# A Fourier mixing layer and a SoLU layer in one kernel: another order of work at its two ends

## The chip, the cores and the metric

The kernel runs on one core of one Trainium2 chip. The metric is the time of one execution on the device, in microseconds (us); the runs of a kernel are given by their median. The core has five engines with a queue of instructions each: TensorE (PE in the profile; its weight loads are PEld), VectorE (DVE), ScalarE (ACT), GpSimd (POOL) and SyncE (SP), which issues transfers. Every engine works through its own queue in the order in which the program puts instructions there, and waits where an instruction needs something that another engine or a transfer has not delivered.

## The reference: what is computed

```python
x:     (8, 3136, 256)                       # batch, sequence, features
X = np.fft.fft(np.fft.fft(x, axis=1), axis=2).real
x = X.reshape(8 * 3136, 256)                # 25088 tokens
h = x @ w_in                                # w_in (256, 1024)
e = np.exp(h - max(h))                      # along the 1024
solu = h * e / (sum(e) + 1e-09)
ln = (solu - mean(solu)) / sqrt(var(solu) + 1e-06) * g_ln
out = ln @ w_out                            # w_out (1024, 256)
```

The weights come as float64 from the host and are taken apart by bits on the chip; all arithmetic is in float32.

## The kernel before, in words

**Tiles and units.** The transform along the sequence is done in two steps (3136 = 49 x 64). The first (`transform1`, L184) multiplies by the table `F` and keeps its result in DRAM (`keep`, L221); `turn` (L224) brings it back with other rows on the partitions, as `g`. The second (`transform2`, L232) multiplies a piece of `g` by the table `T`. Batches are taken in four pairs, and each pair has 25 frequencies `k1`; a pair with a `k1` is a *unit*, so there are 100 units. A unit is 128 tokens and, by symmetry of the real transform, also the 128 tokens of the mirrored frequency: two *signs*, 0 and 1. Units with `k1` of 0 have only sign 0. The transform along the features is not computed: its matrix is multiplied into `w_in` beforehand (`product_in`, `keep_in`), with an even half (`Wi[:, 0]`), an odd half (`Wi[:, 1]`) and one row for the middle feature (`w_mid`).

**One unit.** `take2` (L246) copies the second transform from PSUM to `q`. `up(t, 0)` and `up(t, 1)` (L272) multiply `q` by the even and the odd half, into the PSUM tiles `h0` and `h1`, of which there is one each. `even` (L280) adds, on VectorE, the middle row times the column `t.r`; that column is a row of `q` turned on its side, either by a small transfer (`spread`, L250) or by a matmul (`column`, L265). `join` (L286) makes h of a sign from the even and odd parts and finds its maximum; `expo` (L294, ScalarE) takes exponentials; `product` (L302, VectorE) multiplies by h and sums; `square` (L309, ScalarE) sums squares and writes its result over h; `stats` (L316, ScalarE) and `power` (L332, GpSimd) give the factor 1/sqrt(var). The tiles `h` have two buffers, so the join of a sign waits for the square of the same sign one unit earlier (where both units have two signs).

**Down.** The product with `w_out` needs the unit's u turned. Units 0 to 3 (`WHOLE = 4`, L35) are turned by TensorE (`turn_whole`, L384), in four PSUM banks, which ScalarE and VectorE copy to `uT`. Later units are turned in blocks of 32 by VectorE (`turn_both`, L375), and transfers move the blocks (`move_blocks`, L401, by SP). The product itself runs five units behind (`lag = 5`, L825). For units with two signs it is done with seven block products instead of eight (class `Down`, L453: `p1` to `p7`), for which `sums` (L438, GpSimd) prepares four block sums of u and `weight_sums` (L421, GpSimd) four of `w_out`; `seed`, `keep_p`, `keep_x`, `keep_c` (ScalarE) and `finish` (VectorE) scale and combine. Units with one sign take a plain product (`down`, L513, and `scale`, L527). `store` (L531) writes sign 0 by SP and sign 1 by an indirect transfer of GpSimd.

**Centring.** The mean of `ln` is removed by taking the mean row from `w_out`: `centre` (L694) sums the 1024 rows with sixteen matmul records against a tile of ones, ScalarE scales the sum to `wbar` (L699), and VectorE subtracts it from all of `Wo` (L700).

**Weights.** `w_in` comes in four pieces and `w_out` in four; for each, `exponent` (L573) cuts out the exponent on VectorE, `confine` (L583) clips it, on ScalarE by three instructions or, with `here=True`, on VectorE by two, and `narrow` (L597) puts the float32 number together on VectorE.

**The order around the change** is written by hand (`manual_schedule`, L742); each engine's queue follows the program.
- L773-799: eight chunks of the first pair: load, add the mirrored rows, fold the features (VectorE), `transform1` (TensorE), a copy to `z` (ScalarE, L217).
- L801-824: `turn` of the first five `k1`, the rest of the weights, `transform2` and `take2` of units 0 and 1 with their `spread`, the rest of `keep`, the second table.
- L859-903: units 0 to 4. `begin(i + 1)` (L841) puts `up`, `column` for units 2 and 3, `even` and the next `transform2` into the queues in the middle of unit i. For the next pair `ahead` (L708) loads chunks, adds mirrored rows on GpSimd in halves, behind the last `product` of a unit given by `after` (`behind`, L719), and folds them on VectorE.
- L912-993: units 5 to 99 and five more rounds that only drain.

## Time and profile before

| what | us |
|---|---|
| median of 3 runs (lowest, highest) | 1136.63 (1136.53, 1139.17) |
| the profiled execution's own time | 1132.91 |
| its span in the profile | 1130.9 |
| TensorE busy in the span | 1092.3 |
| VectorE, ScalarE, GpSimd busy | 987.4, 800.5, 796.3 |
| TensorE in the first 47 us | 22.95 |
| TensorE's last matmul ends | 1125.8 |

The profile is of one execution. Its span starts and ends with the first and last instruction; the execution's own time is 2.0 us longer. The granted TensorE clock is 1.0. In a line of a timeline stand the start and the length in us, the engine, the line of the kernel, the operation, output and inputs, the shape, and in brackets how long the engine was idle before and what ended that. A float32 matmul leaves two records, so four records of 128x512 are the two matmuls of one `up`.

### The profile page before, as it was taken

How to read it: one execution, taken by the hardware profiler on the slowest of the kernel's cores; microseconds unless marked ns; L12 is line 12 of the kernel's file. 1: busy time of each engine (PE TensorE's matmuls, PEld its weight loads, DVE VectorE, ACT ScalarE, POOL GpSimd, SP SyncE). 2: the span in 40 equal slices, each digit the busy share in tenths (PEclk: the TensorE clock that was granted, in tenths of full speed). 3: DMA queues.
4: the chain of work that ended last, by engine and by line, in shares of the span. 5: the costliest groups of instructions: out<-in, count | busy, mean ns of one | idle time of the engine just before them, and what ended most of it. 6: DMA issues, size and time to landing. Idle time of an engine off the chain costs nothing.

```text
span 1130.9 us, 21944 instructions
## 1 busy us (share of the span) xinstructions
PE 1092.3 (97%) x7030; PEld 872.2 (77%) x7030; DVE 987.4 (87%) x1442; ACT 800.5 (71%) x1945; POOL 796.3 (70%) x698
## 2 busy tenths in 40 slices
PE   2898999999999999999999999999999999999998
PEld 1556787887887787878877787878877788778888
DVE  7889989898889998898988998898888899898983
ACT  4667777777767777777767777777776777777761
POOL 3036888875795988865878788876686576766673
PEclk9999999999999999999999999999999999999999
DMA  9672798766998879876969798876788685965665
GB/s 246 207 196 57 169 189 205 174 150 147 165 207 159 188 174 186 192 152 144 169 149 186 170 191 187 197 178 148 152 160 156 132 164 116 161 142 112 140 135 119
DMA packets 459601, 185.77 MB, mean 164 GB/s; under 512 B 426870, under 2 KB 441470, under 8 KB 459488
## 3 DMA queue, kind: packets, MB, share of 16 engines
q1 hardware_dynamic: 445728, 146.22, 63.0%
q0 software_dynamic: 13760, 38.16, 13.1%
q8 instruction: 57, 0.93, 0.3%
q14 instruction: 56, 0.46, 0.1%
HBM read 44.78 MB, written 38.80 MB: 74 GB/s over the span
## 4 chain that ended last, share of the span: by engine, by line
PE 90%; DVE 4%; issue 2%; ACT 2%; DMA 2%; SPq 0%; POOL 0%; POOLq 0%; DVEq 0%; ACTq 0%
PE ps_m L451 52%; PE ps_h L277 28%; PE ps_m L214 5%; PE ps_m L242 4%; DMA raw_in<-in_moe_w_in_dram 1%; DVE h L291 1%; DVE u L306 1%; PE ps_m L519 1%; ACT h L313 1%; DVE ev L283 0%; DVE y L150 0%; PE wps L665 0%; DVE Wo L615 0%; DVE y L149 0%; ACT u L299 0%
## 5 line engine op out<-in xcount | busy, mean ns | idle before, releaser
L277 PE MATMUL ps_h<-Wi,q 128*128 128x512 f32 x800 | 362.4, 594 | 5.9 <-DVE nmax L291 5.1
L444 POOL TENSOR_TENSOR S<-uT 128x512 f32<-128x512 f32 x186 | 238.0, 1279 | 108.3 <-DVE u L306 34.5
L451 PE MATMUL ps_m<-Ws,S 128*128 128x128 f32 x2304 | 296.4, 275 | 0.0
L451 PEld LDWEIGHTS ps_m<-Ws,S 128*128 128x128 f32 x2304 | 279.8, 192 | 3.6 <-issue 0.4
L313 ACT ACTIVATE h<-u,usum 128x1024 f32<-128x1024 f32 x196 | 225.3, 1150 | 79.5 <-DVE u L306 79.0
L277 PEld LDWEIGHTS ps_h<-Wi,q 128*128 128x128 f32 x800 | 143.8, 190 | 152.0 <-issue 139.4
L306 DVE SCALAR_TENSOR_TENSOR u<-h,u 128x1024 f32<-128x1024 f32 x196 | 234.7, 1234 | 9.4 <-ACT u L299 9.4
L299 ACT ACTIVATE u<-h,nmax 128x1024 f32<-128x1024 f32 x196 | 223.8, 1143 | 6.0 <-DVE nmax L291 4.7
L377 DVE STREAM_TRANSPOSE v<-u 128x2048 f32<-128x2048 f32 x88 | 203.4, 2311 | 3.1
L451 PE MATMUL ps_m<-Wo,uT 128*128 128x128 f32 x1536 | 203.7, 276 | 0.0
L451 PEld LDWEIGHTS ps_m<-Wo,uT 128*128 128x128 f32 x1536 | 187.9, 192 | 1.0 <-issue 1.0
L291 DVE CUSTOM_DVE_ANT_0 h<-ev,ps_h 128x1024 f32<-128x1024 f32 x100 | 122.2, 1222 | 17.0 <-DVE ev L283 8.8
L536 POOL DMA_INDIRECT out_dram<-ot,idx x96 | 109.7, 1143 | 37.4 <-issue 12.5
L291 DVE CUSTOM_DVE_ANT_0 h<-h,ps_h 128x1024 f32<-128x1024 f32 x96 | 117.2, 1221 | 14.2 <-DVE nmax L291 0.5
L283 DVE SCALAR_TENSOR_TENSOR ev<-w_mid,r,ps_h 128x1024 f32<-128x1024 f32 x100 | 124.1, 1241 | 0.8 <-PE ps_h L277 0.7
L444 POOL TENSOR_TENSOR S<-uT,S 128x512 f32<-128x512 f32 x93 | 118.8, 1278 | 7.3
L444 POOL TENSOR_TENSOR S<-S,uT 128x512 f32<-128x512 f32 x93 | 118.7, 1277 | 7.3
L451 PE MATMUL ps_m<-Wo,S 128*128 128x128 f32 x768 | 101.5, 275 | 0.8 <-ACT ot L486 0.8
L451 PE MATMUL ps_m<-Ws,uT 128*128 128x128 f32 x768 | 101.8, 276 | 0.0
L242 PEld LDWEIGHTS ps_m<-T,g 128*128 128x128 f32 x400 | 60.1, 191 | 50.1 <-issue 45.7
L451 PEld LDWEIGHTS ps_m<-Wo,S 128*128 128x128 f32 x768 | 93.4, 192 | 1.0 <-issue 1.0
L214 PE MATMUL ps_m<-y,F 98*100 98x258 f32 (+3 forms) x288 | 70.4, 377 | 24.4 <-DVE y L162 22.1
(103 smaller groups left out, 1177.7 us busy)
## 6 DMA issues: line engine op xcount, KB each, us to landing
uT<-v SPq DMA_DIRECT2D x752, 128.0 KB
g<-zd POOLq DMA_DIRECT2D x72, 160.0 KB, 5.2
out_dram<-ot SPq DMA_DIRECT2D x176, 64.0 KB
xa<-in_x_dram SPq DMA_DIRECT2D x28, 392.0 KB
zd<-z SPq DMA_DIRECT2D x24, 400.0 KB
raw_in<-in_moe_w_in_dram SPq DMA_DIRECT2D x4, 512.0 KB
raw_out<-in_moe_w_out_dram SPq DMA_DIRECT2D x2, 1024.0 KB
room<-in_x_dram SPq DMA_DIRECT2D x4, 392.0 KB
```

What stands on the lines that cost most here:

```text
L214: nc.tensor.matmul(o[..., cs], F[:, 2 * t + h, :], i[..., cs], start=first, stop=True, skip_group_check=True)
L242: nc.tensor.matmul(o, g[:, k, h * P : (h + 1) * P], table, start=(h == 0), stop=True, skip_group_check=True)
L277: nc.tensor.matmul(ps[:, fs], t.q[:, c * P : (c + 1) * P], Wi[:, c, fs], start=True, stop=True)
L283: nc.vector.scalar_tensor_tensor(out=t.ev, in0=w_mid, scalar=t.r, in1=ps, op0=ALU.mult, op1=ALU.add)
L291: nc.vector.tensor_tensor_reduce(out=t.h[s], in0=t.h[0] if s else t.ev, in1=t.odd, scale=1.0 if s else -0.5, scalar=3.0e38, op0=ALU.add, o ...
L299: nc.scalar.activation(out=t.u[s], in_=t.h[s], func=ACT.Exp, bias=t.nmax[:, s : s + 1], scale=-1.0, accum_out=t.esum[:, s : s + 1])
L306: t.last = nc.vector.scalar_tensor_tensor(out=t.u[s], in0=t.h[s], scalar=-1.0, in1=t.u[s], op0=ALU.mult, op1=ALU.mult, accum_out=t.usum[:, ...
L313: nc.scalar.activation(out=t.h[s], in_=t.u[s], func=ACT.Square, bias=t.usum[:, s : s + 1], scale=-float(FF), accum_out=t.ssq[:, s : s + 1])
L377: nc.vector.transpose(out=t.batch.v[:, :, t.w], in_=t.both.rearrange("p s (g n) -> p (s g) n", n=32))
L444: i = engine.tensor_tensor(out=S[j], in0=a, in1=b, op=op)
L451: nc.tensor.matmul(o, a[:, c], b[:, c], start=start and c == 0, stop=c == n - 1, skip_group_check=True)
L536: dma = nc.gpsimd.indirect_dma_start(out=out, out_offset=bass.IndirectOffsetOnAxis(ap=idx[:, i : i + 1], axis=0), in_=t.ot[s], in_offset=None)
```

## The change

It touches only the two ends of the program. In the queues:

- *Chunks.* In the last chunk VectorE takes two exponents of `w_out` instead of three, clips the first itself and narrows the first piece at once; the clipping of the second is done by ScalarE, one instruction ahead of each of the two copies of that chunk and one behind. `product_in(1)` is cut into four pieces: one after chunk 4, one after chunk 5, two after `turn`.
- *Before unit 0.* Both second transforms of units 0 and 1 (in two PSUM banks) come before the last clipping and the last three narrowings.
- *Mean row.* `fold_out` lets GpSimd add halves of `Wo` three times, 2048 columns to 256; `mean_out` is one matmul with ones on that, in round 1; `keep_mean` scales it on ScalarE behind the exponentials of unit 1; `centre` subtracts on GpSimd in four pieces, behind unit 1's last product. `weight_sums` moves to round 2, behind unit 2's last product.
- *ScalarE.* The turned unit 0 is copied behind unit 1's exponentials; `stats` of a unit moves one round later, behind the next unit's exponentials (units 0 and 1 both in round 2), and `power` to the end of that round.
- *Unit 5.* Its even part is finished by TensorE: two further matmuls with one row (`w_mid[0:1]`) add to the same PSUM tile, and ScalarE copies it to `ev`; this happens in round 4, and unit 5 has no `spread`.
- *Block sums of unit 1.* Two in round 3, two in round 4, instead of all in round 5. The additions of mirrored rows in rounds 3 and 4 stand behind the current unit's product.
- *Tail.* In round 100 the squares and `stats` of unit 99 come behind `keep_c`, its `power` in round 101; four of the sixteen moves of unit 98 are issued by GpSimd; for unit 99 `p7` and its half of `finish` come before `p3`.

The core of the diff:

```diff
+MIDDLE = (5,)
@@ column, up, even
-        ps = result(2)[:, 0:1]
+        ps = result(5 - t.k1)[:, 0:1]
...
+        whole_even = c == 0 and t.p == 0 and t.k1 in MIDDLE
...
+        if whole_even:
+            for half in range(2):
+                fs = slice(half * HW, (half + 1) * HW)
+                nc.tensor.matmul(ps[:, fs], t.q[0:1, P : 2 * P], w_mid[0:1, fs], start=False, stop=True)
...
+        if t.p == 0 and t.k1 in MIDDLE:
+            nc.scalar.copy(t.ev, ps)
+            return
@@ class Weights
-        def centre(self):
-
-            cs = result(0)[:, 0:D]
-            for c in range(KF):
-                nc.tensor.matmul(cs, ones, Wo[:, c, :], start=(c == 0), stop=(c == KF - 1))
-            nc.scalar.mul(out=wbar, in_=cs, mul=1.0 / FF)
-            nc.vector.tensor_tensor(out=Wo, in0=Wo, in1=wbar.unsqueeze(1).to_broadcast([P, KF, D]), op=ALU.subtract)
+        def fold_out(self):
+
+            half = Ws[:, 0:2].rearrange("p j c k -> p (j c k)")
+            quarter, eighth = [Ws[:, j].rearrange("p c k -> p (c k)") for j in (2, 3)]
+            w = Wo.rearrange("p c d -> p (c d)")
+            for o, i in ((half, w), (quarter, half), (eighth[:, 0:D], quarter)):
+                n = o.shape[1]
+                nc.gpsimd.tensor_tensor(out=o, in0=i[:, 0:n], in1=i[:, n : 2 * n], op=ALU.add)
+            self.part = eighth[:, 0:D]
+
+        def mean_out(self):
+            self.cs = result(3)[:, 0:D]
+            nc.tensor.matmul(self.cs, ones, self.part, start=True, stop=True)
+
+        def keep_mean(self):
+            nc.scalar.mul(out=wbar, in_=self.cs, mul=1.0 / FF)
+
+        def centre(self, t):
+
+            for c in range(0, KF, 2):
+                i = nc.gpsimd.tensor_tensor(out=Wo[:, c : c + 2], in0=Wo[:, c : c + 2],
+                                            in1=wbar.unsqueeze(1).to_broadcast([P, 2, D]), op=ALU.subtract)
+                if c == 0:
+                    behind(i, t)
@@ chunks and before unit 0
-                for i in range(3):
+                for i in range(2):
                     weights.exponent_out(i)
+                confine(weights.units[0], True)
+                weights.narrow_out(0)
...
+                if c == NC - 1:
+                    confine(weights.units[0], parts=(s,))
                 transform1(first, c * CH // 2 + s)
...
+        weights.product_in(1, (2, 3), odd)
         middle = weights.product_in(KD)
-        confine(weights.units[0], True)
-        for i in range(1, 3):
-            confine(weights.units[i])
+        confine(weights.units[0], parts=(2,))
+        for i in range(2, 4):
+            weights.exponent_out(i)
+        weights.keep_in(1, odd)
+        confine(weights.units[1])
         weights.keep_in(KD, middle)
...
+        for t, ps in [(t, transform2(pairs[0], t.k1, t.k1)) for t in units[:2]]:
+            take2(t, ps)
+            spread(t)
+        confine(weights.units[2])
         for i in range(1, 4):
             weights.narrow_out(i)
+        weights.fold_out()
@@ units 0 to 4
-                turn_whole(prv)
+                turn_whole(prv, i == 1)
+            if i == 1:
+                weights.mean_out()
...
+            if i == 1:
+                weights.keep_mean()
+            if i in (1, whole):
                 for o, ps in prv.wait:
                     nc.scalar.copy(o, ps)
...
+            done = units[0 if i == 2 else i - 1 : i] if i > 1 else []
+            for t in done:
+                stats(t)
+            if i == whole:
+                nxt = units[i + 1]
+                enter(i + 1)
+                even(nxt, up(nxt, 0))
...
             if i == 1:
-                weights.centre()
-                weight_sums()
+                weights.centre(cur)
+            if i == 2:
+                weight_sums(cur)
...
+            if i == whole - 1:
+                sums(units[1], None, part=slice(0, 2))
+            for t in done:
+                power(t)
@@ units 5 to 99 and the tail
-            if i == len(units):
-                for s in prv.signs:
-                    square(prv, s)
-            if prv:
+            if prv and cur:
                 stats(prv)
...
                     scale(old, s, ps)
+            if i == len(units):
+                for s in prv.signs:
+                    square(prv, s)
+                stats(prv)
...
-            if seven:
+            if seven and old is units[-1]:
+                new.p7()
+                new.finish(1)
                 new.p3()
+                new.finish(0)
...
-                move_blocks(batches[-1], slice(w, w + 1), (nc.sync, nc.gpsimd) if w else (nc.sync,))
+                move_blocks(batches[-1], slice(w, w + 1), (nc.sync, nc.gpsimd) if w else (nc.sync,) * 3 + (nc.gpsimd,))
+                if w:
+                    power(units[-1])
```

## The prediction, made before the changed kernel ran

> **What bounds the kernel now.** I read the chain of waits first, then the busy time by stretches, then each engine's timeline in the opening and at the end. On the page:
>
> ```profile
> span 1130.9 us, 21944 instructions
> PE 1092.3 (97%) x7030; PEld 872.2 (77%) x7030; DVE 987.4 (87%) x1442; ACT 800.5 (71%) x1945; POOL 796.3 (70%) x698
> ...
> PE 90%; DVE 4%; issue 2%; ACT 2%; DMA 2%; SPq 0%; POOL 0%; POOLq 0%; DVEq 0%; ACTq 0%
> ```
>
> TensorE bounds the whole. The busy time by stretches (PE, PEld, DVE, ACT, POOL, granted clock, DMA share, GB/s):
>
> ```profile
> 59.00:109.00 50.00, 44.36 (x196) 27.86 (x195) 45.42 (x66) 37.45 (x81) 23.87 (x23) 1.00 0.49 119
> 109.00:1092.00 983.00, 980.93 (x6438) 792.25 (x6437) 875.97 (x1250) 721.62 (x1789) 742.31 (x638) 1.00 0.79 165
> 1092.00:1131.00 39.00, 32.94 (x288) 32.45 (x286) 18.02 (x31) 11.84 (x31) 18.39 (x21) 0.99 0.53 123
> ```
>
> From 109 us to 1092 us TensorE idles 2.1 of 983, so an edit pays only before and after. Between, the order of work is not touched. In the opening the limit is another one. VectorE's timeline (start, duration, work):
>
> ```profile
> 58.98 1.27 DVE L283 SCALAR_TENSOR_TENSOR ev<-w_mid,r,ps_h 128x1024 f32<-128x1024 f32 x1
> ...
> 68.74 1.23 DVE L306 SCALAR_TENSOR_TENSOR u<-h,u 128x1024 f32<-128x1024 f32 x1 [1.44 <-ACT u L299]
> ...
> 71.55 2.29 DVE L700 TENSOR_TENSOR Wo<-Wo,wbar 128x2048 f32<-128x2048 f32 x1 [0.43 <-ACT wbar L699]
> 73.76 0.15 DVE L270 COPY r<-ps_m 128x1 f32<-128x1 f32 x1
> 73.95 1.28 DVE L283 SCALAR_TENSOR_TENSOR ev<-w_mid,r,ps_h 128x1024 f32<-128x1024 f32 x1
> ```
>
> The even part (L283) opens each unit. It starts at 58.98, 62.33, 73.95, 81.59, 89.06, 98.80 and 109.41 for units 0 to 6, and between 73.95 and 107 VectorE is hardly ever idle. TensorE follows it, until this line of its timeline:
>
> ```profile
> 80.49 0.68 PE L242 MATMUL ps_m<-T,g 128*128 128x128 f32 x4 [0.42 <-DMA g<-zd]
> ...
> 108.72 1.11 PE L214 MATMUL ps_m<-y,F 98*100 98x258 f32 x4 [0.36 <-ACT q L248]
> ```
>
> At 108.72 it waits for the last time in the opening (take2 of unit 8, behind the squares of unit 5). So I follow the change up to that matmul. At the end:
>
> ```profile
> 1098.16 1.13 PE L451 MATMUL ps_m<-Wo,S 128*128 128x128 f32 x8 [0.83 <-ACT ot L486]
> ```
>
> [...] The half fold L149 takes 0.42 us alone; beside the block sums:
>
> ```profile
> 102.73 0.86 DVE L149 TENSOR_TENSOR y<-xa 98x254 f32<-98x254 f32 x1
> 103.52 1.25 DVE L150 TENSOR_TENSOR y<-xa 98x254 f32<-98x254 f32 x1
> ```
>
> L283, with one operand in PSUM, takes 1.28 beside GpSimd and apart from it. [...] Here the same 128x512 sum takes 1.28 us on GpSimd and 0.69 on VectorE (L444 near the end), 1.86 times.
>
> **The change, part by part**
>
> 1. *Before unit 0.* VectorE: four exponents at 0.38, the two confining operations 0.84, four narrowings at 2.64 (pitch of 51.1 to 58.98) from 44.83 give 57.75. The idle 1.12 at 46.71, a wait for the second half of w_out, is gone. But two ScalarE steps of 0.72 now stand between the copies of the last chunk (L217), so its DMA to DRAM leaves 0.72 later, and so does turn's g. In the trace SP's g packets end by 52.75 and TensorE read g at 53.28 without waiting: landing 52.8 to 53.28, after the change 53.5 to 54.0. ScalarE's last three confining steps (0.75 each) stand behind both take2: 55.2 + 2.25 = 57.45, then L610 and two L615, 1.65: 59.1. So the even part of unit 0 starts at 59.1, against 58.98: nothing gained. The pieces of product_in at chunks 4 and 5 (0.9 each) lie mostly in TensorE's gaps of 0.65; 0.1 is left over.
>
> 2. *The mean row.* Eight matmuls (sixteen records, 3.62 us, L698) become one, 0.45. GpSimd's fold_out costs 2.5 + 1.28 + 0.65 from 59.0, done by 63.5; TensorE wants it at 65.8, so it is hidden by 2.3. fold_out stands ahead of the indirect loads of pair 1, which still start sooner than now (63.5, not 67.48). If the cover failed, the matmul would hold up all behind it on TensorE (up and column of unit 2), and keep_mean the copies and squares on ScalarE; keep_mean stands behind expo anyway, which takes the cover to 4.7 us. The subtraction on VectorE, 2.29 with 0.43 of waiting, goes; on GpSimd it is four of 1.28, 69.9 to 75.0, behind unit 1's last product, and nobody needs Wo before the plain product of unit 0 at about 93. Ws follows behind unit 2's product, 78.2 to 83.3, needed near 102.
>
> 3. *ScalarE reordered at units 0 to 2.* Unit 1's exponentials no longer stand behind stats (0.5) and two copies (1.0): the products end at 69.9, not 71.03. So unit 2's even part starts at 73.95 - 1.15 - 2.7 = **70.1**. Then ScalarE must catch up: keep_mean 0.36, copies 1.0, square 1.15, take2 0.35, square 1.25 end at 73.4, and unit 2's second join needs that buffer at 72.7: VectorE loses 0.65. Unit 3: 81.59 - 3.85 + 0.7 = **78.45**. Unit 4, a cycle of 7.5 as now: **86.0** (was 89.06).
>
> 4. *A new late comer.* Unit 5's transform wants g of turn(first, 1), which TensorE had at 80.49; its place is now about 77.4. The DMA engines are full from 57.5 to 80.5 (share 0.8 to 1.1), so g lands as the transfers before it began: spreads and keeps are issued 1.1 us earlier, and the indirect loads, behind power(0) until now, some 4. Bounds: 76.5 to 80.5. VectorE feels it from 78.9, with 1.5 at the worst; I take 0.2.
>
> 5. *Even part of unit 5 by TensorE.* Two more matmuls (four records) with one row. The trace has no such shape; as up is paced by its 512 columns I price the records like the others, 0.43 each, 1.75 (bounds 0.4, if one row were cheap, and 1.75). VectorE loses 1.42 (with the gap behind it), ScalarE gains a copy of 1.0 (L669), TensorE drops nothing, and SP loses one spread (0.5), which nobody misses. The copy waits for up, 87.4 + 3.45, and for ScalarE, 92.8; behind it in ScalarE's queue stand unit 4's squares and stats, take2 of unit 7 and unit 0's scale, so unit 5's exponential starts at 97.9 and the first product could run at 99.2. What hides that is the fold of part 6, which holds VectorE until 99.9[...]. Unit 5's join: 100.21 - 3.05 - 1.42 = 95.7.
>
> 6. *Block sums of unit 1 in halves, mirror behind the current unit.* GpSimd's sums move from 99.07-104.5 to 87.2-90 and 94.4-97. The fold at unit 5 still meets GpSimd (mirror of chunk 1)[...]. power of units 0 to 3 now stands behind weight_sums, mirror and half sums on GpSimd; its first reader is unit 0's scale at 97.4, and it is done by 84.6. turn(first, 2) comes some 3 us earlier, for unit 10. From unit 5's join to unit 6's even part now 9.2[...]: **104.6** (was 109.41), and ScalarE's take2 lets the matmul of 108.72 go at **104.0**. TensorE's own sum agrees: from the end of unit 3's transposes, 87.4, come up even 3.45, odd 1.75, transforms 0.9, plain product 3.46, unit 6's up 3.5, three products and the seed 2.9: 103.4, so the gain can't pass 5.3. Opening: 108.72 - 104.0 - 0.2 = **4.5 us**.
>
> 7. *The tail.* The squares of unit 99 (ScalarE, 1094.56 to 1096.95) no longer precede keep_p: the wait goes, 0.83, and with it what it drags along: the step from one unit's products to the next is 7.32 there, 6.25 elsewhere, 1.07. Next late would be unit 99's blocks, whose moves end on SP at 1116.5 and land about 2.6 later, just as TensorE starts there (1118.99, small gaps of 0.2 in all). But four of unit 98's sixteen moves leave SP for GpSimd, which has time, 2.8 us. Swapping p7 and p3 lets the slow store (indirect, 0.77 to start, landing 3.0) begin 0.9 earlier; the SP store, now last, moved its packets within 1.5 us of issue, so it ends before. 1.07 + 0.1 + 0.9 = **2.1 us**.
>
> Sum: 4.5 + 2.1 = 6.6. The profiled execution took 1132.91 (span 1130.9 and 2.0 around it) and would take 1126.3; the runs' median is 1136.63, 3.7 above it, so I carry over the difference: 1136.6 - 6.6 = **1130.0**.
>
> **Rivals**
>
> - *The opening's gain is eaten [...].* Only the first GpSimd operation of centre and weight_sums is put behind a product, and none of the half sums. In my times weight_sums ends 0.2 before unit 3's product, the half sums just at the fold of unit 4. Two such meetings at 1.3, plus g at its worst (1.3 more), leave 0.7 of the opening: 1136.6 - 0.7 - 2.1 = 1133.8, within measurement. For it: 102.73 above. [...]
> - *The tail gives nothing*, because unit 99's blocks land no earlier and TensorE's wait only moves: 1132.1. Against: the four moves.
> - *Slower[...].* If the new phase between GpSimd's sums and mirrors and VectorE's products at unit 6 persisted, the toll would be paid some 75 times. VectorE is busy 876 of the 983 us there, so about 1.2 us per unit of 11 is spare; from 1.2 + 0.09 (6.6 over 75) it decides. At 0.13 above the slack, 75 times: 1130.0 + 9.8 = 1139.8. Against: from unit 6 the order and the fences are the same, and now too the steady part begins with a meeting, which TensorE doesn't feel.
> - *It doesn't do what it says*: the narrowing isn't sooner (part 1). That is in the forecast.
>
> **How the numbers follow.** Forecast 0.66, opening eaten 0.14, tail lost 0.10, slower 0.07; 0.03 for more than I count. The forecast's own range is 1128 to 1132.5. Below, TensorE's limit of 5.3 and a tail of 2.2 give 1129.1, and the three runs differ by up to 2.6, so 1127. Above, to take in the eaten opening, 1134. A measurement tells about 0.3%, 3.4 us, from no change: faster 0.79, same 0.14, slower 0.07.
>
> **What would show it.** Right: the mean row's sum is one matmul; even parts near 59.1, 70.1, 78.5, 86; TensorE's last wait of the opening near 104; no wait for ScalarE near 1092; the last SP store behind the last indirect one. Wrong: unit 0 starting later than 59.5, a transform waiting on g past 79, folds or products of over 1.5 us on VectorE in units 2 to 5, or TensorE below 10 of 10 after 110.

## The result, and the profile after

In six runs of each, the new kernel took a median of 1134.15 us (1132.82 to 1136.69) and the old one 1137.72 us (1134.00 to 1141.25): ratio 0.9971, 95% interval 0.9948 to 0.9994. A second comparison (22 runs against 27, E6 below) gave 0.9977, interval 0.9967 to 0.9988. The change saves about 3 us (3.6 and 2.5 by the medians), about half of the 6.6 us forecast, and 1134.15 lies just above the range of 1127 to 1134.

The profiled execution of the new kernel took 1132.82 us, and the page begins:

```profile
span 1131.1 us, 21930 instructions
PE 1092.3 (97%) x7020; PEld 874.2 (77%) x7020; DVE 983.0 (87%) x1440; ACT 799.2 (71%) x1946; POOL 807.5 (71%) x709
```

That is the span of the old kernel's profile (1130.9), although the medians differ. So one pair of profiles can't be subtracted here: the old profile, 1132.91 us, was close to the lowest of all runs of the old kernel (1132.67 to 1144.42). I therefore took more profiles of each version and compare stretches of them. The same three stretches as before (columns: busy time of PE, PEld, DVE, ACT, POOL, then granted clock, DMA share, GB/s):

```profile
59.00:109.00 50.00, 43.29 (x182) 27.93 (x181) 42.76 (x66) 38.51 (x83) 33.95 (x30) 0.93 0.53 127
109.00:1092.00 983.00, 980.04 (x6435) 791.82 (x6435) 874.16 (x1248) 718.56 (x1786) 739.61 (x637) 1.00 0.79 164
1092.00:1131.10 39.10, 33.77 (x298) 33.44 (x296) 19.03 (x33) 12.79 (x32) 22.05 (x26) 0.98 0.55 128
```

The first row is the surprise: the clock of TensorE, 1.00 before, is 0.93 there. VectorE's timeline shows that the opening began as forecast and had lost its lead by unit 4's even part (L292 was L283):

```profile
59.94 1.27 DVE L292 SCALAR_TENSOR_TENSOR ev<-w_mid,r,ps_h 128x1024 f32<-128x1024 f32 x1
...
70.97 1.28 DVE L292 SCALAR_TENSOR_TENSOR ev<-w_mid,r,ps_h 128x1024 f32<-128x1024 f32 x1
...
79.08 1.28 DVE L292 SCALAR_TENSOR_TENSOR ev<-w_mid,r,ps_h 128x1024 f32<-128x1024 f32 x1
...
90.67 1.27 DVE L292 SCALAR_TENSOR_TENSOR ev<-w_mid,r,ps_h 128x1024 f32<-128x1024 f32 x1
```

From unit 2's even part to unit 3's it took 8.11 us, from there to unit 4's 11.59. TensorE's timeline gives the reason (L243 was L242, L215 was L214):

```profile
82.41 1.20 PE L243 MATMUL ps_m<-T,g 128*128 128x128 f32 x4 [4.06 <-DMA r<-q]
94.97 1.98 PE L283 MATMUL ps_h<-w_mid,q 1*128 1x512 f32 x4
109.49 1.03 PE L215 MATMUL ps_m<-y,F 98*100 98x258 f32 x4
```

The transform for unit 5 waited 4.06 us for its g, where the old kernel waited 0.42. (In this profile the wait is put down to a small transfer, r; in another profile of the same kernel, E11 below, to g itself.) And after that wait TensorE ran at half its clock:

```profile
78.02:81.43 3.41, 0.32 (x1) 0.00 (x0) 3.20 (x5) 1.78 (x5) 2.24 (x2) 1.00 0.96 187
81.43:84.84 3.41, 2.44 (x11) 2.47 (x12) 0.33 (x2) 1.20 (x2) 3.41 (x5) 0.50 0.37 101
84.84:88.26 3.42, 3.42 (x13) 2.64 (x12) 2.52 (x4) 2.49 (x7) 0.56 (x1) 0.50 0.02 5
88.26:91.67 3.41, 3.41 (x14) 1.84 (x13) 3.30 (x5) 3.07 (x9) 0.84 (x1) 1.00 0.00 0
```

In the third row PE is "busy" all the time, but slowly: the sixteen transposes behind the wait take 3.62 us here and 1.91 in a profile that kept its clock (E6). Only the clock column tells. (Why the rows are cut at these times is said below, under when the clock fell.) GpSimd's timeline shows what went out ahead of g (L128 is the gather of the mirrored rows of pair 1, two of them):

```profile
60.11 2.36 POOL L719 TENSOR_TENSOR Ws<-Wo 128x1024 f32<-128x1024 f32 x1 [6.41 <-DVE Wo L632]
...
64.83 1.86 POOL L128 DMA_INDIRECT xb<-in_x_dram,idx  x1 [0.19 <-issue]
66.99 0.99 POOL L128 DMA_INDIRECT xb<-in_x_dram,idx  x1 [0.30 <-issue]
```

The old kernel issued them at 67.48 and 68.85. In either kernel all of their 0.80 MB (the software queue) moves between 64 us and unit 5's transform. At the end of the kernel the wait of 0.83 us near 1098 is gone, as forecast.

**Reading the opening in all profiles.** Unit 0 starts anywhere from 58.98 to 63.52 us, with the loads of the weights, so I count from its even part. "Transform" is that of unit 5, "last" is the last waiting matmul of the opening (take2 of unit 8). All in us:

| from unit 0's even part to | forecast | old kernel, four profiles | new kernel, three profiles | gathers late (E2, E9, E10) |
|---|---|---|---|---|
| even part of unit 2 | 11.0 | 14.95 to 15.40 | 11.03 | 11.02 to 11.03 |
| even part of unit 3 | 19.35 | 22.58 to 23.03 | 19.13 to 19.14 | 19.12 to 19.13 |
| transform, start | 18.3 | 20.9 to 23.3 | 21.3 to 22.5 | 18.2 |
| even part of unit 4 | 26.9 | 30.04 to 30.73 | 28.20, 29.73, 30.73 | 26.58 to 26.60 |
| last | 44.9 | 49.68 to 50.37 | 45.96, 47.86, 49.55 | 44.34 to 44.35 |

The third row is the finding: in the new kernel the even parts ahead of the transform come 3 to 4 us earlier, and TensorE is done with all that stands ahead of it 18.4 us after unit 0 instead of 21.1 (first profiles), but the transform itself comes no earlier than before.

### The profile page after: what moved, and what is told of

Read it like the earlier page. It is cut to its first block, busy times and chain, and to the rows that moved or that the text cites. A ratio compares the mean times of both kernels' runs of the same rounds, so it can differ in the third digit from the quotient of the medians.

```text
span 1131.1 us, 21930 instructions
## 1 busy us (share of the span) xinstructions
PE 1092.3 (97%) x7020; PEld 874.2 (77%) x7020; DVE 983.0 (87%) x1440; ACT 799.2 (71%) x1946; POOL 807.5 (71%) x709
## 3 DMA queue, kind: packets, MB, share of 16 engines
q0 software_dynamic: 13888, 38.42, 13.3%
## 5 line engine op out<-in xcount | busy, mean ns | idle before, releaser
L292 DVE SCALAR_TENSOR_TENSOR ev<-w_mid,r,ps_h 128x1024 f32<-128x1024 f32 x99 | 122.8, 1241 | 1.5 <-PE ps_h L279 0.8
L243 PEld LDWEIGHTS ps_m<-T,g 128*128 128x128 f32 x400 | 60.5, 192 | 53.8 <-issue 45.9
L143 POOL TENSOR_TENSOR xa<-xa,xb 98x510 f32<-98x510 f32 (+1 forms) x48 | 59.5, 1240 | 50.8 <-DVE u L315 43.0
L462 PEld LDWEIGHTS ps_m<-Ws,uT 128*128 128x128 f32 x768 | 93.8, 192 | 0.0
```

Source lines behind the costliest of these rows:

```text
L143: i = engine.tensor_tensor(out=a[:, :, 1:D], in0=a[:, :, 1:D], in1=rb[:, :, D - 1 : 0 : -1], op=ALU.add)
L243: nc.tensor.matmul(o, g[:, k, h * P : (h + 1) * P], table, start=(h == 0), stop=True, skip_group_check=True)
L292: nc.vector.scalar_tensor_tensor(out=t.ev, in0=w_mid, scalar=t.r, in1=ps, op0=ALU.mult, op1=ALU.add)
L462: nc.tensor.matmul(o, a[:, c], b[:, c], start=start and c == 0, stop=c == n - 1, skip_group_check=True)
```

## The experiments

**Theory A**: the gathers of pair 1, ahead of g in time but in another queue, share the transfer engines with the transfers ahead of g and with g itself; g lands no earlier than before, and TensorE, now early, waits for it and then pays in clock. **Rivals**: g is late for another reason (the plain loads, the keeps themselves); the clock alone is the loss; the tail gave nothing; the loss is chance.

**E1 and E2: the loads out of the way of g.** E1 moves all four loads of pair 1's first two chunks (the plain ones on SyncE, the gathers on GpSimd) from round 0 to round 1:

```diff
-            if work == "load" and (i == (pr.p - 1) * NK and c < 2 or a == 2 and c + 2 < NC):
+            if work == "load" and (i == ((pr.p - 1) * NK or 1) and c < 2 or a == 2 and c + 2 < NC):
```

E2 moves the two gathers alone (load_b is the indirect DMA of load, cut out of it for these two):

```diff
                 other_pairs(i, ahead, work, cur)
+            if i == 1:
+                for c in range(2):
+                    load_b(pairs[1], c, pairs[1].raw[c][1])
```

Expected of E1: 

> The changed kernel, but the first two chunks of the second pair are loaded in round 1 instead of round 0, on SP and on GpSimd. In the changed kernel TensorE waits 4.06 us for the transfer of g before unit 5's transform (82.41 us), then runs 6.5 us at half the granted clock. Theory A (the loads share the DMA engines with what goes ahead of g, above all GpSimd's two, which now leave at 64.8 us): g lands before 78.5, no wait there, clock 1.0, unit 4's even part at 86.5 to 87.5 instead of 90.67, the last wait of TensorE in the opening near 105, and 4 to 5 us less than the changed kernel: ratio to the kernel before about 0.993. Rival B (g is late only because the keeps leave no earlier than before): g lands at 80 to 82 all the same, less than 2 us gained. [...]

Expected of E2: 

> The changed kernel, but only GpSimd's two indirect loads of the second pair move from round 0 to round 1, behind the subtraction; SP's two loads stay. If GpSimd's loads alone are the cause: as the run with both loads late, no wait at unit 5's transform, unit 4's even part near 87. If SP's own loads, which stand behind g in its queue, share with g too: g lands at 79 to 80.5, a wait of 1 to 2 us is left and unit 4's even part is at 88 to 89. If neither: 90.7.

Measured: E1 1130.88 us, ratio 0.9938 (0.9916 to 0.9960); E2 1129.66, ratio 0.9933 (0.9908 to 0.9958). E2's transform on TensorE's timeline, without a wait, and the stretch around it (L247 is L243 of the new kernel):

```profile
78.85 0.61 PE L247 MATMUL ps_m<-T,g 128*128 128x128 f32 x4
```
```profile
77.00:80.00 3.00, 3.00 (x15) 1.93 (x16) 2.96 (x7) 2.94 (x9) 2.25 (x3) 1.00 0.60 153
```

TensorE is busy throughout and keeps its clock. E1 and E2 have the same opening to 0.02 us, so the plain loads, which E1 moves too, add nothing that TensorE notices. The transform comes 3.1 to 4.2 us sooner than in the new kernel (18.2 against 21.3 to 22.5); as TensorE no longer waits, g may have landed sooner still. For comparison, 0.80 MB at the 198 GB/s that the new kernel moved from 64 to 83 us would be 4.0 us (an estimate).

The rival of the keeps (that g is late because its zd is written late) can be settled by when SyncE issues g. The new kernel and E2:

```profile
69.13 2.48 SPq L231 DMA_DIRECT2D g<-zd  x4
```
```profile
70.16 1.76 SPq L235 DMA_DIRECT2D g<-zd  x4
```

That is 9.2 us after unit 0's even part in the first (9.2 to 9.8 in the three profiles) and 9.5 in the second: not later. From there to the transform it is 12.2 to 13.3 us in the new kernel and 8.7 with the gathers late. And the bytes agree: from SyncE's first keep to the transform the transfer engines moved 5.27 to 5.39 MB in the four old profiles, 5.36 to 5.38 in the three new ones, and 4.80 in E2, E9 and E10, which leave the gathers for later. The same bytes stood ahead of g before the change and after it. (The new kernel moved them at 212 to 221 GB/s, the old one at 222 to 231; why is not known.) Theory A stands.

**E3: the clock alone.** Four useless matmuls of 512 columns ahead of unit 5's transform, nothing else changed:

```diff
         ps = result(bank)[:, 0 : KD * P]
+        for n in range(4 if pr.p == 0 and k1 == 5 else 0):
+            nc.tensor.matmul(result(bank), ident, Wi[:, 0, 0:HW], start=True, stop=True, skip_group_check=True)
```

Expected: 

> The changed kernel with four matmuls of no use (128x512, into the bank that the transform then overwrites) ahead of unit 5's transform, so that TensorE works while it waits for g. The landing of g is not touched. Theory: about half of the loss is the granted clock of 0.5 that follows the idle time. Then the clock stays at 1.0, the transform still starts at about 82.4, the sixteen transposes behind it take 1.9 us and not 3.62, unit 4's even part is at 88.5 to 89 and not 90.67, and the time falls by about 2 us. Rival: the clock has another cause or VectorE is late anyway; then unit 4's even part stays at 90.7 and the time is the same.

Measured: 1132.67 us, ratio 0.9959 (0.9946 to 0.9971). The clock stays at 1.00 from 78 to 91 us; unit 4's even part comes 29.28 after unit 0's and the last waiting matmul 47.04. The first profile of the new kernel, where g came as late (transform at 22.5, here 22.4), has 30.73 and 49.55: 1.45 and 2.5 us more, which is the clock's part. The other part, 2.7 us to the 26.58 and 44.34 of E2, is the wait itself. That the clock alone is the loss is thereby refuted. The time of E3 isn't clear of the new kernel's (the intervals overlap), so the split rests on these profiles alone.

**E4: unit 98's moves back on SyncE alone.**

```diff
-                move_blocks(batches[-1], slice(w, w + 1), (nc.sync, nc.gpsimd) if w else (nc.sync,) * 3 + (nc.gpsimd,))
+                move_blocks(batches[-1], slice(w, w + 1), (nc.sync, nc.gpsimd) if w else (nc.sync,))
```

Expected: 

> The changed kernel, but all sixteen moves of unit 98 are issued by SP again. In the changed kernel the last indirect store is issued at 1126.56, 0.5 us earlier than before instead of 0.9, because the store ahead of it leaves GpSimd at 1123.41 (1120.38 before) and each waits for the landing of the one ahead. Theory: the four moves on GpSimd push the stores back; without them the store ahead leaves at about 1120.5 and the last one 0.3 to 0.4 earlier, and the span ends 4.4 to 4.6 us after TensorE's last matmul, not 5.3: some 0.8 us. Rival: the blocks of unit 99 then land late and TensorE waits up to 1 us more ahead of its last unit, so that nothing is gained.

Measured: 1134.35 us, ratio 0.9969 (0.9956 to 0.9982), the new kernel's own time. Both halves of the expectation came: the span ends 4.4 us after TensorE's last matmul (4.9 to 5.5 in the new kernel's three profiles), and TensorE waits 1.07 us ahead of unit 99's products, which is within what the new kernel shows itself (0.15, 0.43 and 1.31). The four moves on GpSimd are worth nothing that these runs can see. That a store waits for the landing of the one ahead stands in the first profile of the new kernel: the landings end at 1119.05, 1122.56 and 1125.80, and the next store goes out 0.76 to 0.87 us later (1119.92, 1123.41, 1126.56).

**E5, E11, E12, E15, E6: more profiles of both kernels**, unchanged.

Expected of E5 (old): 

> The old kernel as it is, for a second profile. Theory A (the early gathers of the new kernel are what makes unit 5's g late): as in the first profile of the old kernel TensorE waits under 1 us for g ahead of unit 5's transform, its clock stays at 1.0 between 76 and 92 us, unit 4's even part begins 29 to 31 us after unit 0's and the last matmul of the opening (line 214) 49 to 51 us after it; one wait of about 0.8 us stands ahead of unit 95's products. Rival: the old kernel meets the same late g in its ordinary runs and the first profile was a lucky one; then the wait is over 2.5 us, the clock falls to about 0.5 for some microseconds and the last matmul of the opening comes 52 us or more after unit 0's even part.

Expected of E12 (old): 

> The old kernel as it is, a third profile. Theory: wait for g of 0.4 to 2 us at unit 5's transform, no fall of the clock, unit 4's even part 30 to 31 us after unit 0's; near 355 us TensorE loses under 0.5 us, one wait of 0.8 us ahead of unit 95's products. Rival (the loss near 355 us is the old kernel's too): 1 us or more lost there.

Expected of E6 (new): 

> The new kernel as it is, on the chip of the two versions beside it. Theory A: ratio to the old kernel 0.996 to 0.999, a wait of 3 to 4.5 us for g ahead of unit 5's transform with the clock at about 0.5 after it for 5 to 7 us, unit 4's even part 29 to 31 us after unit 0's, as in its first profile. Rival (the wait is a chance of the one profiled run): a wait under 1 us and unit 4's even part 26.5 to 27.5 us after unit 0's.

Expected of E11 (new): 

> The new kernel as it is, a third profile. Theory: wait for g of 2.5 to 4.5 us at unit 5's transform; where it is above about 3 us the clock falls to 0.5 after it and unit 4's even part is 28.5 to 31 us after unit 0's, where it is under 3 us the clock stays and it is 27.5 to 28.5. Near 355 us TensorE loses a further 0.4 to 3.3 us behind the block sums. Rival for the second place (it was bad only in one profile): loss there under 0.5 us.

Its border of about 3 us is an estimate, between the wait of 2.90 us that kept the clock (E6) and that of 3.39 that lost it (E4).

E5 took 1135.26 us, E12 1136.49, E11 1134.18 (one run each), E6 a median of 1133.45 (ratio above). The old kernel waits for g too, when its transfers run late (E5):

```profile
83.25 0.68 PE L242 MATMUL ps_m<-T,g 128*128 128x128 f32 x4 [1.79 <-DMA g<-zd]
```

but it loses only some 0.25 us by it: its last waiting matmul is 0.65 us later than in the others (50.37 against 49.73), and 0.43 of that is there at unit 2 already, ahead of the wait. The new one waits 2.90 us in E6 and 3.58 in E11. In E6 the clock holds and unit 4's even part is at 28.20; in E11 the clock is 0.5 from 83.4 to 86.8 and it is at 29.73. The table above holds these numbers.

Behind the opening I compared the starts of VectorE's transposes (STREAM_TRANSPOSE of v) unit by unit. Between two profiles of these kernels they come back to one distance, within 0.2 us, from about 140 us on (passing delays of up to 1.4 us undo themselves within a few units; lasting steps are 0.4 or 0.5 us in E1 and E11 and about 1 us in E3 and E4), save at one place near 355 us, where TensorE comes to the block products of a unit before GpSimd is done. The idle time there was 0, 0.41 and 0.64 us in the first three old profiles, 0.72, 2.25 and 1.48 in the new, 0.64, 2.39 and 1.09 in E2, E9 and E10. I took that at first for a second cost of the change. E15 was to tell.

Expected of E15 (old): 

> The old kernel as it is, a fourth profile, for the place near 355 us. Theory C (the change makes that place worse): TensorE idles under 0.7 us there, as in the three profiles of the old kernel so far (0, 0.41, 0.64). Rival (chance): 1 us or more, as in most profiles of the new one.

Measured: 1136.04 us in its one run, and the rival holds. GpSimd and then TensorE in the old kernel:

```profile
349.36 1.51 POOL L444 TENSOR_TENSOR S<-uT 128x512 f32<-128x512 f32 x1 [4.40 <-DMA out_dram<-ot]
...
353.69 2.09 POOL L444 TENSOR_TENSOR S<-uT 128x512 f32<-128x512 f32 x1
355.75 2.02 POOL L368 TENSOR_TENSOR rs<-mix,neg_half 128x4 f32<-128x4 f32 x1
```
```profile
358.67 1.69 PE L451 MATMUL ps_m<-Ws,S 128*128 128x128 f32 x8 [1.90 <-POOL rs L368]
```
```profile
355.66:359.07 3.41, 1.51 (x13) 1.35 (x13) 3.38 (x3) 2.64 (x9) 3.17 (x4) 1.00 0.73 148
359.07:362.48 3.41, 3.41 (x18) 3.41 (x17) 2.74 (x5) 1.34 (x7) 2.22 (x2) 0.50 0.85 189
```

The sums wait for a transfer (put down to a store of the output; that it is the landing of the blocks is my reading), TensorE waits for GpSimd, and the clock is halved for 3.4 us more: the old kernel loses 3.0 us there in this run, against its first profile. So this place is one of the sources of scatter in both kernels (old: 0, 0.4, 0.6, 3.0 us; new: 0.4, 1.1, 3.3). With so few profiles a small cost of the change there isn't excluded, but the loss as such is not of its making, and it is why single profiles mislead here.

**When the clock fell.** Waits of 3.39 (E4), 3.58 (E11) and 4.06 us (first profile) ahead of unit 5's transform lost the clock and one of 2.90 (E6) did not, yet near 355 us 1.90 (E15) to 2.39 us (E9) were enough. The traces order this. The stretches of half clock that end before the last matmul lasted multiples of 3.41 us: 3.4 in E4, E8, E11 and E15, 6.8 in the first profile of the new kernel, 10.2 in E13, 13.7 in E7. In the first profile the two falls begin 307 times 3.413 us apart (81.44 and 1129.32). So I cut a trace into stretches of 3.413 us that end where its falls begin; the rows above are such stretches. The stretch ahead of a fall had TensorE busy for 0.09 of it in the first profile, for 0.38 in E8 and for 0.44 in E15; a share of 0.49 (E6) was followed by none. (One share of 0.44 without a fall is at the end of E6, and the busy times are modelled.) E6 shows how 2.90 us were survived, with shares of 0.66 and 0.49:

```profile
77.08:80.49 3.41, 2.25 (x7) 0.93 (x6) 3.38 (x7) 3.35 (x10) 0.40 (x1) 1.00 1.06 193
80.49:83.90 3.41, 1.67 (x15) 1.70 (x16) 2.07 (x3) 1.29 (x4) 3.33 (x3) 1.00 0.61 152
```

Its wait (79.33 to 82.23) fell across the edge of two stretches, while the 1.90 us of E15 lay, with smaller gaps, in one (0.44). The clock came back behind a stretch in which TensorE was busy throughout (3.42 of 3.42 us in the first profile, third row, 3.41 of 3.41 in E15, second row) and not behind one of 0.71 (first profile, second row, hence 6.8 us). This is read from traces taken for other ends, from 28 us on, and no run was made to try it. Ahead of 28 us the clock column can't be used: it says 1.00, but eight records of 98x258 take 3.73 us there and 1.94 later (old kernel).

**E14: the late loads in the old kernel**, E1's edit to it.

Expected: 

> The old kernel with the loads of pair 1's first two chunks in round 1 instead of 0. Theory A in its full form (the bytes ahead of g land when they landed before the change; the old TensorE comes to unit 5's transform just as they do and loses little, the new one comes about 4 us sooner and loses it): g is now early here too, but the old kernel gains only its own wait, 0.2 to 1.8 us: ratio 0.9985 to 1.0, unit 4's even part still 29.5 to 30.1 us after unit 0's, the last waiting matmul 49 to 49.8 after it. Rival (the late loads are an improvement of their own, apart from the change): the old kernel gains 3 us or more, ratio 0.9975 or less.

Measured: 1137.66 us, ratio 1.0004 (0.9990 to 1.0018); unit 4's even part 30.04 after unit 0's, the last waiting matmul 49.70. The old kernel gains nothing: its own pace brings TensorE to the transform at 20.9, when g has landed anyhow. The cure is worth some 4 us, but only behind the change.

**E8: the gathers earlier still**, right behind GpSimd's four moves of g, at 54.25 and 55.61 us. In the first profile of the new kernel the transfer engines carried 41 GB/s on average from 54 to 58 us.

```diff
         turn(first, 0, nc.gpsimd, 2, KG)
+        for c in range(2):
+            early_xb[1, c] = xpool.tile([PR, CH, D], FP32, tag="xb", name="xb")
+            load_b(pairs[1], c, early_xb[1, c])
```

Expected: 

> The new kernel with GpSimd's two gathers for pair 1 put right behind its four moves of g at 51 to 54 us, ahead of the fold of w_out: 10 us earlier than in the new kernel, at a time when the transfer engines are nearly idle (0 to 32 GB/s between 55 and 58 us). Theory A in its form that the gathers hurt by sharing the engines with the keeps, the table and g: they are largely through before the keeps begin, so the wait at unit 5's transform is under 1 us, the clock stays at 1.0, unit 4's even part comes 26.5 to 28 us after unit 0's, and the time is that of the late gathers, ratio 0.992 to 0.995. Rival (any gather earlier than the old kernel's hurts, since its bytes stand in the software queue ahead of something that the opening needs): wait of 2.5 us or more, unit 4's even part over 29 us after unit 0's, ratio 0.996 or more.

Measured: 1130.55 us, ratio 0.9953 (0.9935 to 0.9971). No wait at unit 5's transform, so it is the sharing of the engines at the wrong time that hurts, not an early gather as such. But unit 1's even part came 5.02 us after unit 0's instead of 3.42: TensorE's clock fell to 0.5 from 62.4 to 65.8, behind another wait of 2.11 us (1.42 in E2; it was busy for 0.38 of the stretch before the fall). Counted from unit 1's, all else is as in E2 to 0.1 us. Whether the gathers cause that fall or it is chance, this one profile doesn't tell.

**E7, E9, E10: the tail.** E7 is E2 with unit 98's and 99's moves on SyncE and ScalarE in turn, none on GpSimd:

```diff
-(nc.sync, nc.gpsimd) if w else (nc.sync,) * 3 + (nc.gpsimd,)
+(nc.sync, nc.scalar)
```

Expected: 

> The new kernel with GpSimd's two gathers for pair 1 in round 1, and besides the moves of units 98 and 99 on the queues of SyncE and ScalarE in turn, none on GpSimd's. Theory (in the tail GpSimd's own moves, 0.61 us each, push back the indirect stores that stand behind them, and these are spaced by about 3.5 us because each waits for the landing of the one ahead): no wait over 0.3 us ahead of unit 99's products, the stores of units 97 and 98 issued 1 to 3 us earlier against TensorE's last matmul, the span ending 4.2 to 4.6 us after the last matmul instead of 5.2, and 1.0 to 1.8 us less time than the version with the late gathers alone: ratio to the old kernel 0.990 to 0.993. Rival (the queues are not what spaces the stores or lands the blocks; sixteen moves take the same time wherever they are issued): ratio 0.993 to 0.9945, the last store where it was.

Measured: 1150.18 us, ratio 1.013 (1.011 to 1.015): slower, by neither theory. SyncE's queue, and its waits in the last 70 us (us in total, times, longest):

```profile
1079.15 5.75 SPq L426 DMA_DIRECT2D uT<-v  x7
...
1100.33 8.87 SPq L426 DMA_DIRECT2D uT<-v  x9
```
```profile
SPq L426 <- DMA uT<-v: 16.1, 2, 15.4
```

SyncE stopped for 15.4 us in the midst of unit 96's and 97's moves and went on 2.3 us after ScalarE's first move was issued (1098.06), and TensorE then idled 11.61 us. What held it isn't visible in the trace, so the cause stays open and E7 says nothing on the question it was made for.

E9 is E2 with the last unit's second products in the old order (p3 ahead of p7), E10 is E2 once more, measured beside it.

Expected of E9: 

> The new kernel with GpSimd's two gathers for pair 1 in round 1, and the last unit's second products in the old order (p3 and finish(0) ahead of p7 and finish(1)). The forecast's seventh step (the indirect store is the long one of the last two, so the swap saves 0.9 us) expects 0.9 us more than the late gathers alone in the same call. Rival (indirect stores stand one behind the other at about 3.5 us, so that the last one is late in either order): within 0.3 us of the late gathers alone, the last indirect store issued 3 us or more after the one ahead.

Expected of E10: 

> The new kernel with the two late gathers alone, once more, as the partner of the version beside it and for a second profile. Theory A: no wait for g at unit 5's transform, unit 4's even part 26.5 to 27 us after unit 0's, and of that gain all but 0.3 to 1.2 us stays past 355 us (where in the profiles so far the block sums of one unit come late on GpSimd): ratio to the old kernel 0.992 to 0.995. Rival (the second loss near 355 us is a matter of chance and takes what the opening gains): 2 to 3.5 us lost there in this profile.

Measured: E9 1131.38 us, ratio 0.9954 (0.9937 to 0.9971); E10 1130.12, ratio 0.9940 (0.9919 to 0.9961). The intervals overlap, and E9's profile had the loss near 355 us in full (3.5 us). In E9 the span ends 5.7 us after TensorE's last matmul, in E10 5.5: the swap is worth some 0.2 us in this pair, not 0.9. Over all profiles of the unchanged kernels the old order ends 5.1 to 5.2 us after it and the new one 4.9 to 5.5, so a gain isn't clear at all. The last four indirect stores were issued at 1115.88, 1119.50, 1123.89 and 1127.04 in E10, 3.2 to 4.4 us apart; what the last one writes was ready 1.4 us before it was issued. In E9 it was ready 0.8 us before.

**E13: the same cure for pairs 2 and 3**, all first loads one round later:

```diff
-            if work == "load" and (i == (pr.p - 1) * NK and c < 2 or a == 2 and c + 2 < NC):
+            if work == "load" and (i == (pr.p - 1) * NK + 1 and c < 2 or a == 2 and c + 2 < NC):
```

Expected: 

> The new kernel with the first two loads of every pair one round later (rounds 1, 26 and 51 instead of 0, 25 and 50), plain load and GpSimd's gather both. It joins the cure of the opening with the same edit at about 320 us, ahead of the place near 355 us where TensorE waits for the block sums. Theory B (near 355 us it is again the 0.8 MB of the gathers that hold up the moves of the blocks, which GpSimd's sums wait for): TensorE's idle time there under 0.5 us, no fall of the clock, 1 to 2 us less time than the late gathers of pair 1 alone: ratio 0.991 to 0.993. Rival (the gathers are not what makes the moves late, or they then meet the moves themselves): idle 0.6 us or more there, ratio 0.993 to 0.996.

Measured: 1142.30 us, ratio 1.0063 (1.0041 to 1.0085). The opening is that of E1 (44.36), but at 330 us GpSimd's mirror begins to wait 17.75 us for the plain load, which SyncE issues only at 342.4, behind sixteen moves of blocks; and TensorE waits behind it:

```profile
348.11 1.26 POOL L143 TENSOR_TENSOR xa<-xa,xb 98x510 f32<-98x510 f32 x1 [17.75 <-DMA xa<-in_x_dram]
```
```profile
350.64 3.78 PE L462 MATMUL ps_m<-Ws,S 128*128 128x128 f32 x16 [9.56 <-POOL S L455]
```

Pair 2's loads have no round to spare. Whether its gathers also delay the moves in the steady stretch stays open, since this edit hit something larger.

The best version is E2, the change with pair 1's two gathers in round 1 (E1 can't be told from it by time): 1129.66 and 1130.12 us in its two comparisons, 7.4 and 6.4 us under the old kernel.

## Why the prediction was right and wrong, by its own steps

1. *Before unit 0*: nothing gained, as forecast. Unit 0 starts at 58.98 to 61.97 us in the old profiles and 59.94 to 60.92 in the new, so 59.1 can be neither confirmed nor refuted to a us.
2. *The mean row*: right. GpSimd's fold took 2.36 and 2.08 us and was done by 64.6, TensorE took the sum at 66.83 without waiting for it, and the subtraction (71.0 to 76.0 on GpSimd) stood in nobody's way. One thing was not forecast: `column` of unit 2 waits 0.78 us for keep_mean to read the bank that both use; its `r` was there before VectorE came to it, so it cost nothing.
3. *ScalarE reordered*: right. 11.03 and 19.13 against 11.0 and 19.35.
4. *The new late comer*: **the step that failed.** It was named, but it counted the gathers' four us as help, and it put g at 76.5 to 80.5 and the cost at 0.2 us. Counted from unit 0 (59.1 in the forecast) that is 17.4 to 21.4; the transform came at 21.3 to 22.5. The slip is in the sentence "g lands as the transfers before it began". Their start didn't set the landing; the bytes to be moved by then did. The gathers' 0.80 MB were among some 5.3 MB before the change and after it, and issuing them sooner takes nothing off that sum. So g came about when it had come before (the transform of the old kernel at 20.9 to 21.5 in three profiles, at 23.3 in the fourth), and TensorE, 2.7 us sooner at its place, waited. Being issued on another queue didn't keep the gathers out of g's way: between the issue of g and the transform 25% of the engines' time went to the software queue in the new kernel, and 3 to 5% with the gathers late.
   The second half of the slip is the price: "VectorE feels it from 78.9, with 1.5 at the worst; I take 0.2". The wait alone cost unit 4's even part 1.6 (E6, 28.20 against 26.58) to 2.7 us (E3), and where the clock fell 2.3 to 4.2 (E4 with 28.86, E11, the first profile). A fall of TensorE's clock had no term in the step at all. In these traces the length of a wait alone doesn't say whether it came: 1.90 us lost the clock in E15, where they lay in one stretch of 3.41 us (busy for 0.44 of it), and 2.90 us across the edge of two kept it in E6 (0.66 and 0.49). That E6 kept it was luck.
5. *Even part of unit 5 by TensorE*: right. Four records with one row took 1.98 us (1.75 forecast; four of `up` with 128 rows take 1.93 to 1.96 in E14), the copy 0.99 (1.0).
6. *Sums in halves*: right, and a little better, once step 4 is mended. With the gathers out of the way unit 6's even part came 44.6 after unit 0's (45.5 forecast) and the last waiting matmul 44.34 (44.9). That is where the step's own limit stands, TensorE's sum of 103.4 or 44.3 after unit 0: in E2 the opening has nothing left but TensorE's work. The fold at unit 5 took 1.03 instead of 0.42, so the meeting with GpSimd cost 0.6 at most.
7. *The tail*: the first term was right, the other two were not. The wait of 0.83 went in every profile of the new kernel, and in the first one 1.06 with it (29.0 us from the last transposes to the last matmul, 30.1 before). But unit 99's blocks became the next late comer, as the second rival had it: TensorE waits for them 0.15, 0.43 and 1.31 us in the new kernel's profiles (in the old 0.48 in one of four, under 0.3 in the others). From the last transposes to the last matmul the new kernel is 0.6 us shorter in the mean. The swap was to save 0.9; E9 puts it at 0.2, because in the new order the last indirect store is issued 3.15 us behind the one ahead, in the three profiles of the new kernel and in E2 and E10, however early its data is ready. Tail: about 0.6, not 2.1, and this failed too.

Sum with what was measured: the opening gains 49.9 - 47.8 = 2.1 us (means of four old and three new profiles), the tail 0.6: 2.7, against 3.6 and 2.5 in the two comparisons. With part 4 mended, as in E2, the opening gains 49.9 - 44.3 = 5.6, and with the tail's 0.6 that makes 6.2; 7.4 and 6.4 were measured, with intervals of about 2.5 us to either side. So of the 3 to 4 us that the forecast had too much, step 4 accounts for 2.4 (4.5 forecast, 2.1 measured) and the tail for 1.5. The third rival (slower in every unit) did not come: from 140 us on the distance between the kernels stays, apart from the place near 355 us and passing delays.

## What to carry to other kernels

When an edit brings an engine sooner to a transfer, ask which bytes must be moved before that transfer lands, over all queues, and not only when it or those ahead of it were issued: here the same 5.3 to 5.4 MB stood ahead of g before the change and after it, and g's reader came no earlier until 0.80 MB were out of the way (the transform at 18.2 us instead of 21.3 to 22.5). Look at the granted clock of the stretch as soon as TensorE has a wait of two to four us, since the price can be half as much again as the wait (E15: 1.90 us of waiting, 3.0 us lost); and before subtracting two profiles, take a second one of each, and count from a common event.

## What the hardware showed that I had not expected

- After 4.06 us without work TensorE's granted clock was 0.50 for 6.8 us (81.4 to 88.3); the matmuls with 128 columns behind it took twice their time. Near 355 us idle times of 1.90 (E15) to 2.39 us (E9) were enough, for 3.4 us of half clock. TensorE was busy for 0.44 of the 3.41 us ahead of the fall in E15; in E6 0.49 was followed by none.
- GpSimd's four-column multiplication (rs) took 1.04, 1.22 or 2.0 to 2.1 us in the same place of different runs, and a block sum 1.22 or 2.09: near 355 us that difference is part of TensorE's wait. Why it doubles wasn't tried.
- Indirect stores of GpSimd that were ready were issued no closer than 3.15 us behind the one ahead (the last two, in five profiles).
- Putting half of the last moves on ScalarE's queue stopped SyncE's queue for 15.4 us (E7), in sixteen moves that took 13 to 14 us in all to issue in the other runs and 30 here.
